# A decode kernel's first weight load in two halves of 64 partitions, from SyncE and ScalarE

## The chip, the core and the metric

The kernel runs on one core of a Trainium2 chip. The time is device microseconds for one execution, as the median of several runs; lower is better. A profile of one execution comes with it, with times of each instruction and of each DMA packet.

The engines are TensorE (PE, matrix products and transposes), VectorE (DVE), ScalarE (ACT), GpSimd (POOL) and SyncE (SP, which only issues DMAs here). Each has its own instruction stream and works it off in order. A DMA is issued by one engine and carried out by 16 DMA engines; when all of it has landed, a semaphore has risen by 16, and whoever needs the data waits for that.

## The reference

One decode step of an attention block with a KV cache, gated by a small MLP. Two sequences (B = 2), one new token each, D = 512, 32 query heads and 8 key/value heads of width 128, 32,768 cached positions, all float32:

```
xn = layernorm(x)                                   # x [2, 1, 512]
q  = xn @ wq                                        # wq [512, 4096]: 32 heads of 128
p  = softmax(q . k_cache * 128**-0.5)               # k_cache [2, 8, 32768, 128]
s  = (p @ v_cache) @ wo                             # v_cache the same shape, wo [4096, 512]
h  = relu(xn @ w1 + b1) ** 2                        # w1 [512, 1792]
g  = silu(h @ w2 + b2)                              # w2 [1792, 512]
out = x + s * g
```

The two caches hold 268 MB each and are read once. The weights are some 24 MB together; wq is 8.4 MB.

## The kernel before

The kernel is written instruction by instruction; each engine's order is the order in the code, and waits are set by hand. `Lane` wraps an engine, `load(lane, dst, src, sem, *marks)` makes the engine wait for the marks and then issues one DMA, and returns the mark that the data's arrival will reach. All issues have the line of that helper, L84.

**Buffers.** In SBUF, `kring` holds three slots of 64 rows per partition for keys (4.2 MB each, two slots for one load of 8.4 MB), `vbuf` one load of values of 8.4 MB. At the start, `vbuf` serves for weights: first wq (`wq_t`, 128 partitions of 64 KB), and when the queries are done, w1 and w2. `kt[0]` and `kt[1]` hold transposed keys; at the start they also hold x, the layernorm's intermediates, and replicated queries.

**Order of the loads.** SyncE issues all large loads in the order of the code and stops at each one whose buffer isn't free:

- wq (L138), without a wait; the first key load, 8.4 MB (L139); half of the second key load, 4.2 MB (L140)
- w1 (L214), when the last query matmul (L210) is done, as it overwrites wq
- the other half of key load 1 (L215), when DVE has transposed the first half of key load 0; w2 (L216); the two halves of key load 2 (L217, L218), each behind a further transpose
- then value load 0 (when the MLP's last matmul is done), key load 3, value load 1, and so on, keys and values in turn, each behind the transposes or the value matmuls that free its buffer; at the end wo.

ScalarE issues four small loads at the start (L164 to L168): x into two partitions of `kt[0]` (behind a memset of it on DVE, L148), b1, b2, and x once more for the last addition. It has no other work before the layernorm's square root (L194).

**The query chain.** When x has landed, DVE does the layernorm (L188 to L196), PE transposes (L200), DVE copies out `xnT` (L201). PE then waits for `xnT` and for wq (L204) and does 64 matmuls (L210). The result is replicated by DVE into `kt[1]` (L227), transposed by PE (L232), copied by ScalarE into `qT` (L235), and POOL makes the first `qz`.

**The main work.** A half of a key load (64 rows in each partition) is transposed by DVE in two instructions (L309) into `kt[0]` and `kt[1]`, and PE multiplies them with the queries (L270). The first transposes wait for the first key load and for the query chain to have let go of `kt[1]` (`q_read`). Softmax follows for each of the 16 pairs of sequence and key/value head, and PE multiplies the probabilities with the values (L280). The MLP's matmuls (L378, L393) stand between the first halves of keys on PE and DVE.

## Time and profile before

| | |
|---|---|
| median of 3 runs | 1303.7 us (1303.65 to 1303.74) |
| span of the profiled execution (first to last instruction) | 1302.6 us |
| PE / DVE / ACT busy | 639.7 / 619.0 / 128.6 us |
| moved by DMA | 561.14 MB in 10,703 packets |
| granted TensorE clock, mean | 0.785 |

For the profiled execution the span is what is known; the median of the runs is 1.1 us above it. In the views that follow, a row of the timeline has the start, the duration, the engine and its line, what is written from what, and in brackets how long the engine stood idle before and what ended that. "SPq" and "ACTq" are the queues' issuing instructions of SyncE and ScalarE. In the rows of DMA issues the last number is the time from issue to landing in us. DMA queue q1 is SyncE's and q10 ScalarE's. A row of the windows has the window, its length, the busy time of PE, PEld, DVE, ACT and POOL with counts, the granted clock, the mean busy share of the 16 DMA engines and the GB/s; a packet is counted at its start, so that shares slightly above 1 occur in short windows.

### The profile page before, as it was taken

To read this page: it belongs to the slowest core of one execution; us is meant where nothing else is said; L and a number is where in the kernel's file an instruction comes from. 1 tells how busy PE (TensorE), PEld (TensorE's weight loads), DVE (VectorE), ACT (ScalarE), POOL (GpSimd) and SP (SyncE) were. 2 spreads that over 40 slices of the span, in tenths; PEclk is the share of its full clock that TensorE was granted. 3 is DMA by queue.
4 is the path that set the end of the run, shared out by engine and by line. 5 is a ranking of instruction groups with operands and counts; after the bars stand their busy time and mean duration, and the time that the engine had idled before them with its cause. 6 is when DMAs were issued, how large, how long until landed. Compare 5 with 4: busy or idle time off the path is not lost.

```text
span 1302.6 us, 10806 instructions
## 1 busy us (share of the span) xinstructions
PE 639.7 (49%) x4710; PEld 175.6 (13%) x4710; DVE 619.0 (48%) x305; ACT 128.6 (10%) x262; POOL 11.9 (1%) x41
## 2 busy tenths in 40 slices
PE   3555444555535455544536543444653444554368
PEld 1111110111101011110101111111110111111014
DVE  2565553436555344655435555343655534455410
ACT  0111011111001011000111101011100101101010
POOL 0000000000000000000000000000000000000000
PEclk9778677878767787777788777678877778877789
DMA  9999999999999999999999999999999999999998
GB/s 419 418 448 423 441 427 435 431 437 433 431 437 427 443 427 441 429 441 427 439 427 437 433 431 437 427 443 427 441 429 441 427 439 427 439 431 429 441 425 356
DMA packets 10703, 561.14 MB, mean 431 GB/s; under 512 B 1199, under 2 KB 1219, under 8 KB 1478
## 3 DMA queue, kind: packets, MB, share of 16 engines
q1 hardware_dynamic: 10656, 560.99, 99.6%
q8 instruction: 6, 0.10, 0.0%
q10 hardware_dynamic: 38, 0.02, 0.0%
q14 instruction: 3, 0.02, 0.0%
HBM read 561.01 MB, written 0.00 MB: 431 GB/s over the span
## 4 chain that ended last, share of the span: by engine, by line
DMA 77%; DVE 12%; issue 10%; PE 1%; SPq 0%; DVEq 0%
DMA kring<-in_A_k_cache 73%; DVE kt L309 12%; DMA kring<-in_A_v_cache 2%; DMA kring<-in_A_wo 2%; PE o_ps L280 1%; PE acc_ps L533 0%; PE pj_ps L540 0%; SPq L84 0%; DVEq L308 0%; PE acc_ps L411 0%
## 5 line engine op out<-in xcount | busy, mean ns | idle before, releaser
L309 DVE STREAM_TRANSPOSE kt<-kring 128x4096 f32<-128x4096 f32 x128 | 557.6, 4414 | 449.4 <-DMA kring<-in_A_k_cache 449.4
L270 PE MATMUL ps_s<-kt,qz 128*32 128x512 f32 x2048 | 333.5, 779 | 603.4 <-DVE kt L309 603.4
L280 PE MATMUL o_ps<-vbuf,pTh 128*16 128x512 f32 x1984 | 227.5, 612 | 1.8 <-DMA vbuf<-in_A_v_cache 1.8
L270 PEld LDWEIGHTS ps_s<-kt,qz 128*32 128x32 f32 x2048 | 67.8, 128 | 845.1 <-issue 669.9
L333 ACT ACTIVATE sc<-ps_s,halves 128x512 f32<-128x512 f32 x64 | 46.6, 729 | 866.5 <-PE ps_s L270 866.5
L280 PEld LDWEIGHTS o_ps<-vbuf,pTh 128*16 128x16 f32 x1984 | 57.8, 101 | 178.0 <-issue 158.6
L343 ACT COPY pTh<-pT_ps 64x256 f32<-64x256 f32 x128 | 46.9, 366 | 39.6 <-PE pT_ps L299 21.6
L315 DVE CUSTOM_DVE_ANT_0 sc<-sc 128x1024 f32<-128x1024 f32 x16 | 19.6, 1225 | 54.9 <-ACT sc L333 54.9
L318 DVE CUSTOM_DVE_ANT_0 junk<-mx_ps,other 128x128 f32<-128x128 f32 x16 | 4.7, 292 | 82.1 <-PE mx_ps L288 82.1
L336 ACT ACTIVATE sc<-sc,nm 128x1024 f32<-128x1024 f32 x16 | 18.4, 1149 | 108.9 <-DVE nm L318 108.9
L328 DVE TENSOR_REDUCE hr<-fin_ps 128x4 f32<-128x64 f32 x16 | 3.6, 225 | 48.5 <-PE fin_ps L292 48.5
L292 PE MATMUL fin_ps<-ident,o_sb 128*128 128x128 f32 x64 | 10.5, 286 | 17.4 <-DVE o_sb L485 17.2
L348 ACT COPY o_sb<-o_ps 128x512 f32<-128x512 f32 x15 | 8.8, 586 | 97.2 <-PE o_ps L280 97.2
L299 PE MATMUL pT_ps<-ident,sc 128*128 128x128 f32 x128 | 17.5, 282 | 0.0
L299 PEld LDWEIGHTS pT_ps<-ident,sc 128*128 128x128 f32 x128 | 15.3, 147 | 0.0
L280 PE MATMUL o_ps<-kring,pTh 128*16 128x512 f32 x64 | 9.3, 749 | 9.0 <-DMA kring<-in_A_v_cache 9.0
L493 POOL COPY oT<-ho 128x4 f32<-128x4 f32 x15 | 2.8, 188 | 1147.2 <-DVE ho L329 1147.2
L210 PE MATMUL pT_ps<-vbuf,xnT 128*32 128x512 f32 x64 | 8.5, 693 | 7.4 <-DMA vbuf<-in_A_wq 7.4
L227 DVE COPY kt<-pT_ps 128x512 f32<-128x512 f32 x8 | 5.0, 683 | 13.2 <-PE pT_ps L210 13.2
L540 PE MATMUL pj_ps<-ident 128*128 128x128 f32 x88 | 10.8, 278 | 0.0
L540 PEld LDWEIGHTS pj_ps<-ident 128*128 128x128 f32 x88 | 10.1, 192 | 1.9 <-issue 1.9
L485 DVE TENSOR_TENSOR o_sb<-o_sb,o_ps 128x512 f32<-128x512 f32 x15 | 10.2, 682 | 0.0
(90 smaller groups left out, 105.5 us busy)
## 6 DMA issues: line engine op xcount, KB each, us to landing
kring<-in_A_k_cache SPq DMA_DIRECT2D x4, 4096.0 KB, 23.8
vbuf<-in_B_w SPq DMA_DIRECT2D x2, 3584.0 KB, 28.5
kring<-in_A_wo SPq DMA_DIRECT2D x1, 4096.0 KB, 41.2
kring<-in_A_wo SPq DMA_DIRECT2D x1, 2304.0 KB, 25.5
kring<-in_A_wo SPq DMA_DIRECT2D x1, 1024.0 KB, 27.6
kring<-in_A_wo SPq DMA_DIRECT2D x1, 512.0 KB, 28.4
vbuf<-in_A_v_cache SPq DMA_DIRECT2D x31, 30.1
kring<-in_A_k_cache SPq DMA_DIRECT2D x30, 29.8
```

Of the source, the lines that this page charges most:

```text
L270: i = tensor.matmul(ps_s[32 * g:32 * g + 32, :], qz[:, 2 * y + e, :], kt[y][:, g * NO:(g + 1) * NO, 32 * e:32 * e + 32], start=(y == 0 and ...
L280: mm_ = tensor.matmul(o_ps[32 * g:32 * g + 16, :], pTh[:, 2 * g + c, 2 * i:2 * i + 2, :, :].rearrange("p o y h -> p (o y h)"), vt[:, lo:lo ...
L292: t = tensor.transpose(fin_ps[:, i * P:(i + 1) * P], o_sb[:, i * DH:(i + 1) * DH], ident)
L299: t = tensor.transpose(pT_ps[:, k // 4, (k % 4) * P:(k % 4 + 1) * P], p[:, k * P:(k + 1) * P], ident)
L309: KT[y].after(vector.transpose(kt[y], k_slot(q)[:, :, 64 * y:64 * y + 64]))
L315: return DVE(lambda: vector.tensor_tensor_reduce(scf[0], scf[0], scf[1], 1.0, -3.4e38, ALU.add, ALU.max, rm), mark, on=on)
L333: ACT(lambda: scalar.mul(sc[c][:, :, :, u], ps_s.rearrange("p (o w) -> p o w", w=32), halves[:, c:c + 1]), *marks, on=EV)
L336: return ACT(lambda: scalar.activation(scf[0], scf[0], AF.Exp, bias=nm, scale=SCALE, accum_out=l), mark, on=on)
L343: i = scalar.copy(pTh[64 * a:64 * a + 64, :, :, y, :], v[64 * y:64 * y + 64, :, :, a0, a, :])
L348: scalar.copy(o_sb, o_ps).then_inc(OE.sem, 32)
L485: DVE(lambda: vector.tensor_add(o_sb, o_sb, o_ps), on=OSR)
L540: tensor.matmul(pj_ps[:, 0:P], ident, ident, start=True, stop=True)
```

## The change

The one issue of wq becomes two: SyncE loads partitions 0 to 63, ScalarE partitions 64 to 127, each with a semaphore of its own and without a wait. ScalarE's issue stands ahead of its four small loads. PE waits for both.

```diff
-    wq_in = load(SP, wq_t, wq.rearrange("(p d) f -> p d f", p=P), dma("wq"))
+    HP = P // 2
+    wq_r = wq.rearrange("(p d) f -> p d f", p=P)
+    wq_low = load(SP, wq_t[0:HP], wq_r[0:HP], dma("wq_low"))
+    wq_high = load(ACT, wq_t[HP:P], wq_r[HP:P], dma("wq_high"))
     k0_in = load_k(0)
     load_k_half(1, 1)
...
-    TE.wait(have_xnT, wq_in)
+    TE.wait(have_xnT, wq_low, wq_high)
     q_done = []
```

## The prediction

> **What bounds the kernel now.** I read the page's slices and its DMA queues first, then the chain of waits with its opening window, then the timeline of the first 45 us, and last windows cut by hand over the stream of packets. The page:

> ```profile
> span 1302.6 us, 10806 instructions
> ...
> DMA  9999999999999999999999999999999999999998
> ...
> DMA packets 10703, 561.14 MB, mean 431 GB/s; under 512 B 1199, under 2 KB 1219, under 8 KB 1478
> ...
> q1 hardware_dynamic: 10656, 560.99, 99.6%
> ...
> q10 hardware_dynamic: 38, 0.02, 0.0%
> ...
> DMA 77%; DVE 12%; issue 10%; PE 1%; SPq 0%; DVEq 0%
> ```

> All 16 DMA engines are busy in every slice: 561 MB at 431 GB/s is the span. SyncE's queue, q1, carries it all; ScalarE's, q10, has 38 packets. Nothing can be gained but at the two ends of this stream, and anything that makes the 16 engines carry bytes more slowly, or leaves them without work, is paid in full. Because a load is complete only when its last engine is, one engine that falls behind sets the end.

> The opening, by the timeline, with the rows that the change touches:

> ```profile
> 0.74 0.38 SPq L84 DMA_DIRECT2D vbuf<-in_A_wq  x1
> 1.17 0.90 SPq L84 DMA_DIRECT2D kring<-in_A_k_cache  x2
> 1.43 1.22 ACTq L84 DMA_DIRECT2D kt<-in_A_x  x1
> ...
> 10.34 0.69 DVE L188 TENSOR_REDUCE st<-kt 128x1 f32<-128x512 f32 x1 [7.33 <-DMA kt<-in_A_x]
> ...
> 15.55 0.29 DVE L201 COPY xnT<-mx_ps 128x128 f32<-128x128 f32 x1 [1.22 <-PE mx_ps L200]
> ...
> 22.90 8.52 PE L210 MATMUL pT_ps<-vbuf,xnT 128*32 128x512 f32 x64 [7.38 <-DMA vbuf<-in_A_wq]
> ...
> 31.55 0.33 SPq L84 DMA_DIRECT2D vbuf<-in_B_w  x1
> ...
> 34.46 0.60 PE L232 MATMUL acc_ps<-ident,kt 128*128 128x128 f32 x4
> ...
> 43.30 17.43 DVE L309 STREAM_TRANSPOSE kt<-kring 128x4096 f32<-128x4096 f32 x4 [9.26 <-DMA kring<-in_A_k_cache]
> ...
> 52.10 0.33 SPq L84 DMA_DIRECT2D kring<-in_A_k_cache  x1
> ```

> The reader is to see two chains. The transfers: wq (8.4 MB) is there at 22.9, the first keys at 43.3. The small one: x arrives at 10.34, the layernorm gives xnT at 15.84, and PE then waits 7.38 us for wq. So xnT has 7 us to spare today, and the query work, over at 35.06, has 8.2 us to spare before the keys arrive.

> **The change, part by part.**

> *Issue.* SyncE's one issue of wq (0.38 us) stays, for half the rows; ScalarE gets one more, ahead of its four small loads, at no more than the 1.22 us of x's row. The keys leave SyncE no later. Nothing stands in front: ScalarE does nothing else before 1.43. Two waits replace one at L204. I count these at nothing: the stream is behind them. Most that an earlier start could give is the head before the first packets, which start between 1.6 and 2.1 us (next fence): 2.1 at most, under 0.2%.

> *Bytes.* The same 8.4 MB move, so the question is only the rate.

> ```profile
> DMA packets 16, 1.05 MB, mean 2097 GB/s; under 512 B 0, under 2 KB 0, under 8 KB 0
> ...
> DMA packets 32, 2.10 MB, mean 291 GB/s; under 512 B 0, under 2 KB 0, under 8 KB 0
> ...
> DMA packets 16, 0.79 MB, mean 1985 GB/s; under 512 B 0, under 2 KB 2, under 8 KB 4
> ...
> q10 hardware_dynamic: 4, 0.01, 4.9%
> ...
> 17.00:19.40 2.40, 0.00 (x0) 0.00 (x0) 0.00 (x0) 0.00 (x0) 0.00 (x0) 1.00 1.01 438
> ...
> 180.00:1240.00 1060.00, 511.40 (x3694) 129.27 (x3698) 522.38 (x229) 102.53 (x203) 8.02 (x26) 0.77 1.00 433
> ```

> These are packets that start in 1.6 to 2.1, in 0 to 7.2 and in 7.2 to 7.6 us, then two windows with the rate in the last column. A packet is one partition's 64 KB. Sixteen of them start within half a microsecond, one to an engine; 32 until 7.2, so each engine takes about 2.4 us for one, and wq is eight such rounds. The engines march in step. And x, whose issue ended at 2.65, has no packet on q10 until 7.2: a packet of 2 KB waited until two of 64 KB had ended. So an engine works on one packet at a time, whichever queue it is from, and takes the queues in turn.

> With the change, the 16 engines therefore get: low rows, low rows, then high and low in turn (four each), all engines at the same half at about the same time. Every large load of this trace goes to 128 partitions, and its rate is 433 to 438 GB/s whatever it carries, so no row says whether the engines or the partitions they write set that rate. The price has two ends. If the engines do, a half goes as fast as a whole: nothing. If the way into the partitions does, 64 partitions take half the rate as long as all engines write the same half: 8.39 MB at 433 GB/s are 19.4 us, at half of it 38.7, so plus 19.4. Less than nothing is excluded, beyond the 2.1 us of the head, as the engines never idle. The nearest rows, 16 packets in step and no sharing between queues within an engine, leave no way for the two halves to fill each other's gaps, so I take the upper end. One deduction: an engine that is a little ahead of the one it shares with has its partitions alone for that long. I estimate 0.1 us a round for the pair that is closest, from 16 starts in 0.5 us: 8 x 0.1 = 0.8. The term is **plus 18.6 us**.

> [...] No row here shows a load of 64 partitions. [...]

> *What x pays.* The small loads now stand behind four 64 KB packets of wq on ScalarE's queue. Counting turns on an engine (L L H L H L H, end of L, H, K, end of H, K, x, K, end of x), x's end comes three key packets after wq, 7.3 us, where it came 12 us ahead of it. wq itself counts as landed one key packet late, 2.4 us. Wq lands 22.0 us after its issue, at 22.7 (next fence). From x's landing at 22.7 + 7.3 = 30.0, without the rate loss, L188 to the first matmul take 5.5 + 0.1, the 64 matmuls 8.5 and the rest until 35.06 another 3.7: the query work is over at 47.8 and not at 35.06. That is 4.5 us after the keys' 43.3, so the first transposes go 4.5 us late; with the rate loss both move by 18.6 and the 4.5 us stay. Does DVE's delay leave the engines without work? SyncE's next issues wait for it:

> ```profile
> vbuf<-in_A_wq SPq DMA_DIRECT2D x1, 22.0
> ...
> vbuf<-in_B_w SPq DMA_DIRECT2D x1, 3584.0 KB, 29.9
> ...
> kring<-in_A_k_cache SPq DMA_DIRECT2D x1, 4096.0 KB, 19.0
> ...
> DMA packets 31, 0.52 MB, mean 520 GB/s; under 512 B 15, under 2 KB 15, under 8 KB 15
> ```

> These are wq, w1, issued at 31.55, the second half of key load 1, issued at 52.10 after the first transposes, and the packets that start in 59.0 to 60.0. In that microsecond 15 engines close w1 (15 small packets) and go on to the keys. An issue needs up to 1.4 us to its first packet (0.74 to 2.1), so the one at 52.10 was needed at 57.6 at the earliest: 5.5 us to spare, and 4.5 are used. w1 itself, issued at 31.55 + 12.7 = 44.3, has the keys in front of it until about 50.7 (59.2 less 8.5 for its 3.67 MB at 433): enough. The later waits are looser: in the chain's rows

> ```profile
> 71.23 8.78 DVE kt L309 x2
> ...
> 80.03 19.05 DMA kring<-in_A_k_cache
> ```

> the load issued at 80.03 lands 19 us later though its 4.2 MB take 9.7, so some 8 us are spare there. The delay dies out in them: **0 us**, and up to 2 if the spare 5.5 are less.

> **Sum.** The profiled span 1302.6 + 18.6 = 1321.2; the median shown, 1303.7, is 1.1 above the span, hence **1322.3 us**. Own range: pairs half a microsecond apart in each round, 8 x 0.5 = 4 less than 19.4, give 1319; the full 19.4 and 2 for a gap give 1325. [...]

> **Rivals.**

> *Not slower: the engines set the rate* (0.24). If 2.4 us a packet is an engine's own pace, four low and four high packets take what eight whole ones did, and the rest is covered as worked out: 1303.7, at most 1 us off either way. For it: the rate is the same for every source and packet size, as it would be with sixteen equal engines. It would also come about if each half were dealt to eight engines of its own, whose turns then don't meet. Against it: nothing in the trace, only the step I took above. It decides from the point where a packet into 64 partitions takes 2.4 us beside fifteen others. [...]

> *Partly in step* (0.06). If the shared pairs fall half a packet apart (1.2 us), each round costs 2.4 + 1.2 and not 4.8: plus 9.7, 1313.4. It needs every pair to do so, as the slowest engine counts, and the 0.5 us of the first round speaks against it.

> *The query chain leaves the engines idle* (0.02). If x comes not 7 but 15 us after wq (q10 served rarely beside SyncE's queue), the transposes go 12 us late, the 5.5 spare are gone and 6.5 us are lost beside the rate loss: 1329. x's own rows speak against: it got its turn as soon as a packet ended.

> *The halves don't go together* (0.66 forecast includes it). If ScalarE's issue takes its 1.22 us, two low packets go first; the order above counts that already, and even wholly one after the other the halves cost 38.7 us.

> *Faster* (0.02): by over 0.2%, 2.6 us, only if the trace hides idle time; the head is 2.1.

> **How the numbers follow.** Forecast 0.66, in step at half rate; partly 0.06; not slower 0.24; idle engines 0.02; faster 0.02. A measurement of this kernel can tell some 0.2% (2.6 us) from no change. Slower: 0.66 + 0.06 + 0.02 = 0.74; same 0.24; faster 0.02. The range of 8 in 10 must take in the case of no change: 1303.0 to 1325.

> **What would show it.** Right: in the window from 1.7 us on, the rate is about 215 to 230 GB/s until some 40 us and 433 after it; the first keys land near 62, x near 49, and PE's first L210 then waits for xnT, not for wq. Behind that, the window from 180 us on has its 433 GB/s unchanged. Wrong: a rate of 430 from 1.7 to 22 (the engines set it), or something between (partly). A stretch with a DMA share under 0.9 near 60 to 80 us would show that the covers were mis-sized.

## The result and the profile after

| | before | after |
|---|---|---|
| median of the runs | 1303.65 us (5 runs) | 1323.76 us (5 runs, 1323.61 to 1323.93) |
| span of the profiled execution | 1302.6 us | 1322.3 us |
| ratio | | 1.0155, 95% interval 1.0143 to 1.0166 |

The change makes the kernel 20.1 us slower. First the page of the changed kernel (span, rate in 40 slices, packets, the two queues):

```profile
span 1322.3 us, 10807 instructions
...
GB/s 222 354 438 441 419 438 440 422 438 440 422 438 440 422 438 440 422 438 440 422 438 440 422 438 440 422 438 440 422 438 440 422 438 440 422 438 440 422 437 358
DMA packets 10719, 561.14 MB, mean 424 GB/s; under 512 B 1215, under 2 KB 1235, under 8 KB 1494
...
q1 hardware_dynamic: 10592, 556.80, 98.1%
q10 hardware_dynamic: 118, 4.22, 1.5%
```

The bytes are the same, and the rate is lost in the first slice and part of the second (a slice is 33 us). Windows of the changed kernel cut by hand, DMA share and GB/s in the last two columns:

```profile
9.70:14.50 4.80, 0.00 (x0) 0.00 (x0) 0.00 (x0) 0.00 (x0) 0.00 (x0) 1.00 1.03 218
...
24.20:29.00 4.80, 0.00 (x0) 0.00 (x0) 0.00 (x0) 0.00 (x0) 0.00 (x0) 1.00 1.03 218
...
80.00:100.00 20.00, 10.80 (x66) 2.52 (x62) 10.42 (x6) 0.71 (x1) 0.00 (x0) 0.77 0.98 421
...
200.00:1260.00 1060.00, 512.15 (x3694) 128.75 (x3698) 522.42 (x229) 102.51 (x203) 7.99 (x26) 0.77 1.00 433
```

The share of the 16 DMA engines is about 1 in all four: they are not without work, they are at half speed while wq comes, 218 GB/s against 421 and 433 later. The opening, from the timeline of the changed kernel:

```profile
0.73 0.61 ACTq L84 DMA_DIRECT2D vbuf<-in_A_wq  x1
...
0.74 0.56 SPq L84 DMA_DIRECT2D vbuf<-in_A_wq  x1
...
47.23 0.69 DVE L191 TENSOR_REDUCE st<-kt 128x1 f32<-128x512 f32 x1 [44.21 <-DMA kt<-in_A_x]
...
52.79 8.90 PE L213 MATMUL pT_ps<-vbuf,xnT 128*32 128x512 f32 x64 [0.38 <-DVE xnT L204]
...
64.73 0.60 PE L235 MATMUL acc_ps<-ident,kt 128*128 128x128 f32 x4
...
65.37 17.42 DVE L312 STREAM_TRANSPOSE kt<-kring 128x4096 f32<-128x4096 f32 x4 [1.04 <-PE acc_ps L235]
...
74.17 0.33 SPq L84 DMA_DIRECT2D kring<-in_A_k_cache  x1
```

Lines after the edit are three higher. And the DMA issues of the changed kernel, with the us from issue to landing (both halves of wq, the first keys, the key half issued at 74.17):

```profile
vbuf<-in_A_wq ACTq DMA_DIRECT2D x1, 42.4
vbuf<-in_A_wq SPq DMA_DIRECT2D x1, 42.2
...
kring<-in_A_k_cache SPq DMA_DIRECT2D x1, 60.7
...
kring<-in_A_k_cache SPq DMA_DIRECT2D x1, 4096.0 KB, 17.0
```

Wq is complete at 0.73 + 42.4 = 43.1, where it was at 22.7: 20.4 us later. The keys land at about 62.1 (issued at 1.4), 18.9 later. The first packets of w1, next behind the keys, start at 70.8 and not at 50.7, 20.1 later, and that is also what the whole kernel loses. PE's first query matmul now waits for `xnT` and not for wq, and the first transposes wait for the query chain (PE's L235) and not for the keys.

### The profile page after: what moved, and what is told of

Its sections match the earlier page's. It is cut to its first block, busy times and chain, and to the rows that moved or that the text cites. A ratio compares the mean times of both kernels' runs of the same rounds, so it can differ in the third digit from the quotient of the medians.

```text
span 1322.3 us, 10807 instructions
## 1 busy us (share of the span) xinstructions
PE 644.2 (49%) x4710; PEld 175.3 (13%) x4710; DVE 618.9 (47%) x305; ACT 128.5 (10%) x262; POOL 11.9 (1%) x41
## 2 busy tenths in 40 slices
DMA  9999999999999999999999999999999999999998
DMA packets 10719, 561.14 MB, mean 424 GB/s; under 512 B 1215, under 2 KB 1235, under 8 KB 1494
## 4 chain that ended last, share of the span: by engine, by line
DMA 73%; DVE 14%; issue 10%; PE 3%; ACT 0%; DVEq 0%; SPq 0%
DMA kring<-in_A_k_cache 65%; DVE kt L312 13%; DMA kt<-in_A_x 3%; DMA kring<-in_A_v_cache 2%; DMA kring<-in_A_wo 2%; PE o_ps L283 1%; PE pT_ps L213 1%; PE pj_ps L381 0%; PE ps_s L273 0%; PE acc_ps L536 0%; PE pj_ps L378 0%; ACT L423 0%; ACT sc L339 0%; PE mx_ps L203 0%; DVE sc L318 0%
## 5 line engine op out<-in xcount | busy, mean ns | idle before, releaser
L273 PE MATMUL ps_s<-kt,qz 128*32 128x512 f32 x2048 | 336.9, 786 | 589.3 <-DVE kt L312 589.3
## 6 DMA issues: line engine op xcount, KB each, us to landing
kring<-in_A_k_cache SPq DMA_DIRECT2D x4, 4096.0 KB, 21.8
vbuf<-in_B_w SPq DMA_DIRECT2D x2, 3584.0 KB, 22.4
kring<-in_A_wo SPq DMA_DIRECT2D x1, 4096.0 KB, 41.0
vbuf<-in_A_v_cache SPq DMA_DIRECT2D x31, 29.9
```

The source lines that it names most:

```text
L273: i = tensor.matmul(ps_s[32 * g:32 * g + 32, :], qz[:, 2 * y + e, :], kt[y][:, g * NO:(g + 1) * NO, 32 * e:32 * e + 32], start=(y == 0 and ...
```

## The experiments

The theory: which partitions are written sets the rate, and it is half as high while all engines write into one side of partition 64 (0 to 63, or 64 to 127), as with the 218 GB/s above. The rivals: taking turns between two queues halves the rate; any load of fewer than 128 partitions is slow; a part of the 20 us comes from the late x. All times stand against runs of the kernel before of 1303.6 us on the same chip. Edits are shown against the changed kernel unless another is named, and are cut to the lines that matter.

### Halves of columns in place of partitions

```diff
-    wq_low = load(SP, wq_t[0:HP], wq_r[0:HP], dma("wq_low"))
-    wq_high = load(ACT, wq_t[HP:P], wq_r[HP:P], dma("wq_high"))
+    HD = ND // 2
+    wq_r = wq_r.rearrange("p d f -> p (d f)")
+    wq_c = wq_t.rearrange("p d f -> p (d f)")
+    HW = HD * HQ * DH
+    wq_low = load(SP, wq_c[:, 0:HW], wq_r[:, 0:HW], dma("wq_low"))
+    wq_high = load(ACT, wq_c[:, HW:2 * HW], wq_r[:, HW:2 * HW], dma("wq_high"))
```

> wq in two halves from SyncE and ScalarE again, but halves of the columns: each is 128 partitions of 32 KB. Partitions theory (all engines write the same 64 partitions at a time, which take half the rate): a 32 KB packet takes 1.2 us as in the 4.2 MB key loads, wq is complete near 22 to 24 us and the time is that of the kernel before, 1303.7 within 1. Queues theory (taking turns between two queues is what halves the rate): 2.4 us a packet, 215 GB/s, some 1323. x stands behind wq's half here too and lands near 27 to 30 us in place of 10.3; if the late query chain costs anything of its own, it shows as 1 to 5 us over 1303.7.

Measured: 1303.73 us, ratio 1.0001 (0.9991 to 1.001). From its DMA issues and a window:

```profile
vbuf<-in_A_wq ACTq DMA_DIRECT2D x1, 4096.0 KB, 22.1
vbuf<-in_A_wq SPq DMA_DIRECT2D x1, 4096.0 KB, 21.9
...
11.50:21.50 10.00, 0.00 (x0) 0.00 (x0) 0.00 (x0) 0.00 (x0) 0.00 (x0) 1.00 0.97 419
```

Two queues in turn carry wq as fast as one: it lands after 22.1 us, where it took 22.0. The queues theory falls, and the splitting as such costs nothing. Here too x is late (27.7) and the first transposes start at 45.5 in place of 43.3, without a cost in the time.

### Both halves of 64 partitions from SyncE

```diff
-    wq_high = load(ACT, wq_t[HP:P], wq_r[HP:P], dma("wq_high"))
+    wq_high = load(SP, wq_t[HP:P], wq_r[HP:P], dma("wq_high"))
```

> Both halves of 64 partitions, one behind the other, from SyncE alone; ScalarE's small loads have its queue for themselves. Partitions theory: each packet of both halves takes 4.8 to 4.95 us, wq is complete near 41 to 43 us, and the time is 1322 to 1324. Queues theory: 2.4 us a packet and 1303.7. x's end comes one or two packets after its issue, at 10 to 17 us.

Measured: 1325.01 us, ratio 1.0164 (1.0147 to 1.018), 1.2 us above the changed kernel. A window, the 64 KB packets that start in 16 to 21 us, and two rows of the timeline:

```profile
11.50:21.50 10.00, 0.00 (x0) 0.00 (x0) 2.79 (x6) 0.00 (x0) 0.00 (x0) 1.00 1.03 210
...
q1 hardware_dynamic: 16, 1.05, 102.2%
...
18.53 0.69 DVE L191 TENSOR_REDUCE st<-kt 128x1 f32<-128x512 f32 x1 [15.51 <-DMA kt<-in_A_x]
...
44.34 8.63 PE L213 MATMUL pT_ps<-vbuf,xnT 128*32 128x512 f32 x64 [20.64 <-DMA vbuf<-in_A_wq]
```

One queue is as slow. Here x lands at 18.5, PE waits for wq again, and the time is not better: with x on time the loss stays. The extra 1.2 us don't hide a gain, as wq itself is there 1.2 later (44.3 against 43.1), so the late x is no part of the loss. That x took 18.5 where 10 to 17 was expected fits the slower packets in front of it, 102.2% of 5 = 5.11 us each.

### Partitions 32 to 95, then the outer quarters

```diff
-    wq_low = load(SP, wq_t[0:HP], wq_r[0:HP], dma("wq_low"))
-    wq_high = load(ACT, wq_t[HP:P], wq_r[HP:P], dma("wq_high"))
+    wq_mid = load(SP, wq_t[32:96], wq_r[32:96], dma("wq_mid"))
+    wq_low = load(SP, wq_t[0:32], wq_r[0:32], dma("wq_low"))
+    wq_high = load(SP, wq_t[96:P], wq_r[96:P], dma("wq_high"))
...
-    TE.wait(have_xnT, wq_low, wq_high)
+    TE.wait(have_xnT, wq_mid, wq_low, wq_high)
```

> wq in three loads from SyncE: partitions 32 to 95, then 0 to 31, then 96 to 127. [...] How-many theory (the rate goes with the number of partitions, or any load of fewer than 128 is slow): 4.9 us a packet in the first four rounds too, and 1323 or, if 32 partitions have a quarter of the rate, some 1343.

Measured: 1314.87 us, ratio 1.0086 (1.0069 to 1.0102), 11.2 us more than before. By the theory the outer quarters alone are slow: their 4.2 MB take 9.7 us at 433 GB/s and 9.7 more at half of it. Three windows of the same run:

```profile
1.70:11.50 9.80, 0.00 (x0) 0.00 (x0) 2.04 (x9) 1.28 (x1) 0.28 (x2) 1.00 1.05 429
...
11.50:21.50 10.00, 1.13 (x4) 0.73 (x4) 3.08 (x8) 0.20 (x1) 0.00 (x0) 1.00 0.98 211
21.50:31.50 10.00, 0.00 (x0) 0.00 (x0) 0.00 (x0) 0.00 (x0) 0.00 (x0) 1.00 1.01 210
```

Sixty-four partitions from 32 on go at 429 GB/s; the outer quarters, 32 partitions each, at 211 and 210. So it isn't the number of partitions (64 went at 218 or at 429, and 32 as fast as 0 to 63) but which ones.

### Even and odd partitions

```diff
-    wq_low = load(SP, wq_t[0:HP], wq_r[0:HP], dma("wq_low"))
-    wq_high = load(ACT, wq_t[HP:P], wq_r[HP:P], dma("wq_high"))
+    wq_low = load(SP, wq_t[0:P:2], wq_r[0:P:2], dma("wq_low"))
+    wq_high = load(ACT, wq_t[1:P:2], wq_r[1:P:2], dma("wq_high"))
```

> The change with other halves: SyncE loads the 64 even partitions, ScalarE the 64 odd ones, so each half has partitions from both ends. [...] If a load is dealt to the engines by the partition it writes, or if it is enough that a half spans all of the partitions, 2.4 us a packet and 1303.7.

Measured: 1304.04 us, ratio 1.0003 (0.9994 to 1.0013), the time of the kernel before. The packets that start before 7.2 us, by queue; then the landing of both halves and the window of wq:

```profile
q1 hardware_dynamic: 16, 1.05, 43.5%
q10 hardware_dynamic: 16, 1.05, 33.6%
...
vbuf<-in_A_wq ACTq DMA_DIRECT2D x1, 22.6
vbuf<-in_A_wq SPq DMA_DIRECT2D x1, 22.4
...
1.70:21.80 20.10, 0.00 (x0) 0.00 (x0) 1.31 (x7) 1.28 (x1) 0.28 (x2) 1.00 1.00 417
```

This is the change itself but for one thing, which 64 partitions (with their rows of wq) make a half: same queues, same sizes, 16 packets of each queue in turn. The 20 us are gone: the time is 0.4 us above that of the kernel before. x is late here as well (27.5), and the first transposes start at 45.3 in place of 43.3. How a load is dealt to the engines wasn't seen in any run, so which of the two conditions named before the run was met stays open.

### The small loads ahead of ScalarE's half

```diff
-    wq_high = load(ACT, wq_t[HP:P], wq_r[HP:P], dma("wq_high"))
     k0_in = load_k(0)
...
     biases_in = load(ACT, x4[0:P:Y, :], x2.rearrange("b (j e) -> j b e", j=ND), biases, zero_x4)
+    wq_high = load(ACT, wq_t[HP:P], wq_r[HP:P], dma("wq_high"))
```

> The change as it is, but ScalarE issues its four small loads ahead of its half of wq. Partitions theory: x lands after one to three packets of 4.9 us, 8 to 17 us, PE waits for wq again and not for x, the transposes start as soon as the keys are there, and the time is still 1323 to 1324, as the late chain is covered. Rival: of the 20.1 us some come from the late query chain and its issues; then the time is 1 to 4 us below 1323.8. ScalarE's half starts one or two packets later than with the change, which moves nothing.

Measured: 1356.73 us, ratio 1.0407 (1.0389 to 1.0424). Both theories missed by 33 us. From its DMA issues, timeline and windows:

```profile
vbuf<-in_A_wq ACTq DMA_DIRECT2D x1, 85.4
...
89.51 9.61 PE L213 MATMUL pT_ps<-vbuf,xnT 128*32 128x512 f32 x64 [65.44 <-DMA vbuf<-in_A_wq]
...
24.00:90.00 66.00, 0.56 (x5) 0.23 (x8) 0.29 (x1) 0.00 (x0) 0.00 (x0) 1.00 0.94 229
...
90.00:100.00 10.00, 10.00 (x73) 3.31 (x66) 3.22 (x6) 0.22 (x2) 0.00 (x0) 1.00 0.14 62
```

ScalarE's half took 85 us to land; PE waited 65 us for it, and from 90 to 100 the DMA engines had nearly nothing to do, as the next loads wait for the query matmuls. The order of a few small packets had moved the landing of ScalarE's half from 43.1 to 89.4 us. A new theory: an engine takes one packet from each queue in turn whatever its size, so that each packet of a few bytes ahead of the half lets a 64 KB packet of SyncE's pass. To test it without the loss of rate, the same order with even and odd partitions (the edit is shown against the run with these):

```diff
-    wq_high = load(ACT, wq_t[1:P:2], wq_r[1:P:2], dma("wq_high"))
     k0_in = load_k(0)
...
     biases_in = load(ACT, x4[0:P:Y, :], x2.rearrange("b (j e) -> j b e", j=ND), biases, zero_x4)
+    wq_high = load(ACT, wq_t[1:P:2], wq_r[1:P:2], dma("wq_high"))
```

> Halves of even and odd partitions (no loss of rate), with ScalarE's four small loads ahead of its half, as in e4. Turns theory (an engine gives each queue one packet in turn, and a packet of a few bytes uses up a turn as one of 64 KB does): the engine with most small packets has some eight of them, data and ends, ahead of its four of wq, so its last wq packet comes after about twelve packets of SyncE's: ScalarE's half lands 38 to 44 us after its issue, PE's first matmul is near 42 to 46, the transposes start near 55 to 58, 12 or more late, and beyond the cover of 5.5 the time is 6 to 9 us longer: 1308 to 1313. Rival (in e4 the half rate alone delayed ScalarE's half): it lands by 27, PE waits for it as in the kernel before, and the time is 1303.7 within 1.

Measured: 1311.38 us, ratio 1.006 (1.0043 to 1.0076).

```profile
vbuf<-in_A_wq ACTq DMA_DIRECT2D x1, 39.7
...
43.82 8.99 PE L213 MATMUL pT_ps<-vbuf,xnT 128*32 128x512 f32 x64 [27.82 <-DMA vbuf<-in_A_wq]
...
56.49 17.42 DVE L312 STREAM_TRANSPOSE kt<-kring 128x4096 f32<-128x4096 f32 x4 [1.06 <-PE acc_ps L235]
...
50.00:55.00 5.00, 5.00 (x49) 2.93 (x42) 4.05 (x8) 1.26 (x8) 0.00 (x0) 1.00 0.53 170
```

Landing, first matmul, transposes and time all fall where the turns put them. The trace has the turns themselves: the last of ScalarE's 64 KB packets start in groups near 27.4, 32.2 and 37.0 us, 4.8 us apart, which is one such packet and one of SyncE's, 2.4 us each.

In the run before this one the low rate went on beside the keys until about 90 (229 GB/s from 24 on). The four packets of ScalarE's half that start there between 53.1 and 54.9 us:

```profile
q10 hardware_dynamic: 4, 0.26, 100.2%
```

That is 1.002 x 16 x 1.8 / 4 = 7.2 us for each, three times 2.4. Which packets met there wasn't seen: how the late half and the keys get in each other's way stays open.

### x late, wq whole

The edit is against the kernel before:

```diff
-    x_in = load(ACT, xt[0:Y + 1:Y, :], x2, small, zero_x)
+    x_in = load(ACT, xt[0:Y + 1:Y, :], x2, small, zero_x, k0_in)
```

> The kernel before, with whole wq, but ScalarE waits for the first keys (43.3) before it loads x: the late x of the change without its slow load. x lands near 45 to 48, the query work is over near 65 and the first transposes go 22 us late, 16 beyond the cover of 5.5 that the prediction counted. w1, issued near 62, finds the engines idle since 50.7: about 12 us lost, and the next key half, issued near 74, another 2 to 4. Theory of the cover: 1317 to 1321, nearly the change's time by another way. Rival (DMA engines make up for it or the chain is of no weight at the start): 1304 to 1306.

Measured: 1322.18 us, ratio 1.0141 (1.0124 to 1.0158), 18.6 us more, a little above what was expected. From its timeline and windows:

```profile
48.84 0.69 DVE L188 TENSOR_REDUCE st<-kt 128x1 f32<-128x512 f32 x1 [45.82 <-DMA kt<-in_A_x]
...
67.14 17.42 DVE L309 STREAM_TRANSPOSE kt<-kring 128x4096 f32<-128x4096 f32 x4 [1.04 <-PE acc_ps L232]
...
50.00:55.00 5.00, 1.74 (x8) 0.93 (x12) 2.70 (x7) 0.20 (x1) 0.00 (x0) 1.00 0.02 8
55.00:60.00 5.00, 5.00 (x36) 1.27 (x32) 0.00 (x0) 0.00 (x0) 0.00 (x0) 1.00 0.00 0
```

Nearly the time of the change, and nearly its late x (48.8 and 47.2), but by the other way: here the engines run dry. From 50 to 60 they move almost nothing. The changed kernel lost its time earlier, with a share of 1 and at half rate, while wq came. The transposes are 67.14 - 43.30 = 23.8 late and cost 18.6, so 5.2 us were covered; in the run with even and odd partitions and the small packets first, 13.2 late cost 7.8, so 5.4 were.

## Why the prediction was right, step by step

*The bound.* Right: all of the loss is in the stream, and behind it the rate is 433 GB/s as before.

*The rate of a half.* Right, in place and kind. The step for which the trace of before had no row, that the partitions written set the rate, was a choice between two ends when it was made, at 0.66 to 0.24; the middle and the even partitions bear it out: 429 and 417 GB/s for 64 partitions from both sides of 64, 210 to 218 for 64 from one side. What lies between the engines and the partitions, and makes it so, no run shows.

One rival is left standing. Every run brings a row of wq to the same partition, and the two halves of partitions are also the two halves of wq in one piece each in the DRAM, so where the rows come from moved together with where they go. Against it speaks w1 in the kernel before, 3.67 MB in one piece, less than such a half (4.2 MB), and loaded into all 128 partitions. In this window all but a few bytes are its own:

```profile
51.00:59.00 8.00, 5.40 (x32) 1.24 (x32) 8.00 (x3) 0.72 (x1) 0.00 (x0) 0.71 1.01 438
```

A source in one piece as short as that came at 438 GB/s; it didn't halve the rate by itself. No run loaded the same rows into other partitions, which would settle it.

*Its size.* The term was 18.6 and wq came 20.4 later; the kernel takes 20.1 more. The deduction of 0.8 for engines a little ahead was the author's estimate and wrong: no run shows a gain from being ahead. Beyond the full 19.4 comes a little more, 0.7 us here and, with the median of the one-queue run, 21.4 - 19.4 = 2.0 there. The packets show it: one of 64 KB took 33.6% of 7.2 = 2.42 us with even and odd partitions, 98.7% of 5 = 4.94 in the changed kernel (next fence) and 102.2% of 5 = 5.11 from one queue, where twice 2.42 is 4.84; eight rounds make 0.8 and 2.2. The 0.8 wrongly deducted and this 0.7 are the 1.5 us between the forecast of 1322.3 and the measured 1323.8. Halves in turn are 1.2 us better than one after the other, about 3% of the 42 us.

*The order of turns.* Wrong in one place: "low rows, low rows, then high" should be low, high, low, high from the start. The packets of the changed kernel that start in 0 to 6 and in 6 to 11 us, by queue:

```profile
DMA packets 16, 1.05 MB, mean 175 GB/s; under 512 B 0, under 2 KB 0, under 8 KB 0
...
q1 hardware_dynamic: 16, 1.05, 80.1%
...
DMA packets 16, 1.05 MB, mean 210 GB/s; under 512 B 0, under 2 KB 0, under 8 KB 0
...
q10 hardware_dynamic: 16, 1.05, 98.7%
```

Sixteen of SyncE's, then sixteen of ScalarE's. So x came one packet sooner than counted, at 47.2 and not 48.6, and the transposes 65.37 - 62.1 = 3.3 us after the keys and not 4.5. It changed nothing in the sum.

*The cover of the late query chain.* Right: 5.5 us had been counted, and two runs that outlast it give 5.2 and 5.4. In the changed kernel 3.3 of it are used; the key half issued at 74.17 still waits, landing after 17.0 us where it took 19.0.

*The rivals.* "The engines set the rate" is out, by the change itself and by the middle partitions. It had half a point: halves in turn from two queues cost nothing to speak of (1303.73 us with halves of columns, 1304.04 with even and odd partitions) when each half had partitions from both sides of 64. "Partly in step", plus 9.7, is out as well: the packets in the last fence take the full 4.9 us. "The query chain leaves the engines idle" didn't occur in the change, but it did as soon as the order on ScalarE's queue was another.

## What to carry to other kernels

## What was not expected of the hardware

Small packets were dear in turns. Four loads of 17 KB in all, put ahead of a 4.2 MB half, delayed its landing from 22.6 to 39.7 us after its issue with the rate at 418 GB/s in the first 20 us, which fits each taking a turn against a 64 KB packet of 2.4 us; with the halves of the change the same order made it 85.4.
